# Holding loads behind x, moving all weight conversions behind the spectrum, and giving GpSimd both filter sums, in the opening of a Fourier mixer with a SoLU layer

## The chip, the cores and the metric

The kernel runs on one core of a Trainium2 chip. A core has five engines that each work through their own instructions in order: TensorE (PE; its weight loads are shown as PEld), VectorE (DVE), ScalarE (ACT), GpSimd (POOL) and SyncE (SP), which here only issues DMAs. SP, ACT and POOL issue the DMAs of this kernel; those of POOL are prepared by POOL's own instructions, so they take its time. Sixteen DMA engines carry the data. The metric is device time in microseconds (us), the median of several runs.

## The reference

Everything is float32 but the two weight matrices, which arrive as float64 words.

```python
X = np.fft.rfft(x, axis=1)                   # x: (8, 3136, 256)
y = np.fft.irfft(X * (filt_r + 1j * filt_i)[None], n=3136, axis=1)
t = y.reshape(25088, 256)
h = t @ w_in                                 # w_in: (256, 1024)
solu = h * softmax(h)
ln = (solu - mean(solu)) / sqrt(var(solu) + 1e-6) * g_ln
out = ln @ w_out                             # w_out: (1024, 256)
```

## The kernel before

The transform of 3136 = 49 x 64 points is done by matrix products. For one example: a first product with `wf_t` (L233) over the 49-point part, whose result goes to a scratch tensor `d1` in DRAM to be rearranged; then the spectrum, seven units of up to two residue pairs, each with forward products (L308, tile `pb`), the product with the filter (`multiply`, L329 to L331), inverse products (L308, tile `pc`) and a store to the scratch tensor `d2`; then a product back with `wi_t` (`back`, L404), which leaves `y`. The token layer works on `y` in steps of a hand-written order (`step`): products with `w_in_sb` (L754), the softmax and the products with `w_out_sb` (L885). Examples 1 to 7 are transformed between these steps by the table `PLAN`.

The change lies in the opening, which handles example 0 alone and prepares the weights before step 0 can run. All of it is under a manual schedule: program order is the order on each engine.

- `fetch_x` loads x in eight pieces of four columns. Half 0 (48 rows a piece, and the last row by itself) goes through SP, half 1 (49 rows, reversed) through POOL, each with runs of 4 KB and 1 KB. `begin(0)` and `begin(1)` (raw float64 words of two weight quarters, 512 KB each) stand between them on POOL; the tables `de` and filter rows `f` of the first eight pairs follow (`load_tables`, two sets of nine DMAs).
- After each piece's first product ACT copies it out and it is stored to `d1`: 96 rows by ACT, 4 by SP.
- `idle_row(5)` puts five products that nothing reads ahead of the spectrum. Each is a full float32 product and shows as two PE instructions. They need the first set of tables. One more idle product stands before each unit's inverse, and `idle_row(14)` after the last.
- SP fetches the units' `d1` rows (`t2`) once `d1` has landed; the last two units' are fetched by POOL.
- In `multiply` DVE forms two products from PSUM per part; the difference of part 0 is DVE's, the sum of part 1 is GpSimd's (L331).
- `load_float64` turns one quarter of the weights (128 x 512) into float32: eight DVE instructions, for `w_in` an ACT and a GpSimd product besides, and an addition, on GpSimd but for the last quarter, where it is a ninth DVE instruction. Quarters 0 and 1 are done early; 2 to 7 after the spectrum. `weight_sums(w_in_sb)` (L152) then forms the combined quarters.
- SP loads the `d2` rows back (`t4`, L358), then x of example 1, and stores the filters to `f_dram`.
- Step 0 starts with `product(0, 1)`, `keep` (ACT, L764), `product(0, 2)` and `finish` (DVE, L778). It ends with `prepare_w_out` (L691 to L709). `pair_sums(0)` and the x loads of later pieces stand on POOL in front of it.

The `raw` tiles have five buffers, `power`, `pt`, `pr` and `pi` two each.

Of the kernel before, what the change touches and what calls it, by code (L numbers as in the profile page):

```python
# [9 lines left out]
FP32 = mybir.dt.float32  # L10
# [84 lines left out]
def kernel(  # L95
# [315 lines left out]
    with ExitStack() as st:  # L411
# [13 lines left out]
        def load_float64(dst, raw, negate, share, add=nc.gpsimd.tensor_tensor):  # L425


            lo, hi = raw[:, :, 0], raw[:, :, 1]
            power = wpool.tile([P, 512], I32, name="power", tag="power", bufs=2)
            frac = dst.bitcast(I32)  # L430
            ts, stt = nc.vector.tensor_scalar, nc.vector.scalar_tensor_tensor
            ts(out=lo, in0=lo, scalar1=8, scalar2=None, op0=ALU.logical_shift_right)
            rest = lo.bitcast(FP32)
            ts(out=power, in0=hi, scalar1=20, scalar2=0x7FF, op0=ALU.logical_shift_right,
               op1=ALU.bitwise_and)
            ts(out=power, in0=power, scalar1=896.0, scalar2=0.0, op0=ALU.subtract, op1=ALU.max)
            if negate:
                ts(out=power, in0=power, scalar1=255.0, scalar2=None, op0=ALU.min)
                ts(out=power, in0=power, scalar1=23, scalar2=-2 ** 31, op0=ALU.logical_shift_left,
                   op1=ALU.bitwise_or)  # L440
            else:
                ts(out=power, in0=power, scalar1=255.0, scalar2=2.0 ** 23, op0=ALU.min, op1=ALU.mult)
            stt(out=power, in0=hi, scalar=-2 ** 31, in1=power, op0=ALU.bitwise_and,
                op1=ALU.bitwise_xor)
            ts(out=frac, in0=hi, scalar1=0xFFFFF, scalar2=3, op0=ALU.bitwise_and,
               op1=ALU.logical_shift_left)
            nc.vector.tensor_tensor(out=frac, in0=frac, in1=power, op=ALU.bitwise_or)


            if share:  # L450
                nc.scalar.mul(rest, lo, 2.0 ** -44)
                nc.gpsimd.tensor_tensor(out=rest, in0=rest, in1=power.bitcast(FP32), op=ALU.mult)
            else:
                stt(out=rest, in0=lo, scalar=2.0 ** -44, in1=power.bitcast(FP32), op0=ALU.mult,
                    op1=ALU.mult)
            add(out=dst, in0=dst, in1=rest, op=ALU.add)
# [82 lines left out]
        fetch_x(0, 0, NCH, 0, N1 - 1, nc.sync.dma_start)  # L539
        fetch_x(0, 0, NH, N1 - 1, 1, nc.sync.dma_start)  # L540
        for i in range(pieces):
            if i:
                fetch_x(0, NCH * i, NCH, 0, N1 - 1, nc.sync.dma_start)
# [12 lines left out]
        def idle(out):  # L556

            nc.tensor.matmul(out=out, lhsT=tables[0][0][:, 0, 0].rearrange("p u q -> p (u q)"),
                             rhs=filters[0][0][:, 0], start=True, stop=True)
# [5 lines left out]
        idle_row(5, "idle")  # L565

        def convert(j):
            load_float64(weights[j][0], raws.pop(j), negate=j < 4, share=j < 4,
                         add=(nc.vector if j == 7 else nc.gpsimd).tensor_tensor)

        for j in range(2):
            convert(j)
# [9 lines left out]
        for i in range(1, units - 2):  # L582
            sp.fetch(i, nc.sync.dma_start, spare_piece(i - 1))
            if i == 3:
                load_tables(8, NP - 8, nc.sync.dma_start)
        for i in range(2):
            start(i)
            tables_back(4 * i, 4)
        for i in range(units):
# [4 lines left out]
            sp.multiply(i, 0, nc.vector.tensor_tensor)  # L594
            sp.multiply(i, 1, nc.gpsimd.tensor_tensor)
            pss = [ps_t.tile([P, 2, C], FP32, name=f"pc_0_{i}_{u}", tag="t") for u in range(2)]
            idle(pss[0])
            sp.inverse(i, pss)
            sp.store(i, nc.scalar.dma_start)
            if i == 0:  # L600
                nc.gpsimd.dma_start(out=wi_t, in_=wi_dram)
                nc.gpsimd.dma_start(out=wq_t, in_=wq_dram)
                nc.gpsimd.dma_start(out=wb_t[:, 0:N1], in_=wb_dram)
                nc.gpsimd.dma_start(out=g_sb, in_=moe_g_ln.rearrange("(k p) -> p k", p=P))
            elif i == 1:
                for last_one in (units - 2, units - 1):
                    sp.fetch(last_one, nc.gpsimd.dma_start, spare_piece(last_one - 1))
# [559 lines left out]
```

## Time and profile before

| | |
|---|---|
| runs, median (lowest to highest) | 1599.01 us (1598.26 to 1602.79) |
| profiled execution: span | 1598.0 us; the page gives no other time for it |
| granted TensorE clock, mean | 0.997 |
| busy: PE, DVE, ACT, POOL | 97%, 82%, 57%, 74% |
| first product of example 0 starts / spectrum starts | 11.76 / 43.42 us |
| back starts / step 0's first product | 82.78 / 97.05 us |

The span is 1.0 us below the median of the runs. Starts are counted from the start of the span. In a timeline a line has the start, the time taken, the engine, the line of the kernel, the instruction and what it writes and reads; the brackets hold the idle time before it and what ended that. A DMA line of SPq, ACTq or POOL is the issue alone, not the transfer.

### The profile page before, as it was taken

What the parts mean: (1) busy time and instruction counts of PE and PEld (TensorE: products, weight loads), DVE (VectorE), ACT (ScalarE), POOL (GpSimd) and SP (SyncE); (2) the same over time, 40 slices, a digit from 0 to 9 for tenths busy, and PEclk for the clock granted to TensorE, in tenths of its full rate; (3) what the DMA queues carried; (4) which work ended last, traced back from release to release, by engine and by line L of the source; (5) the groups of instructions that cost most, each with busy time, mean ns of one, the idle gap of its engine ahead of it and who ended that gap; (6) DMA issues with size and microseconds to landing.
All of it is one profiled execution on the core that took longest, in us unless ns stands there. A gap on an engine that the chain in (4) does not pass through costs nothing. (4 is left out here: it accounts for less than half of the span.)

```text
span 1598.0 us, 37061 instructions
## 1 busy us (share of the span) xinstructions
PE 1548.0 (97%) x12828; PEld 1055.5 (66%) x12828; DVE 1310.2 (82%) x2639; ACT 915.8 (57%) x1825; POOL 1177.0 (74%) x1371
## 2 busy tenths in 40 slices
PE   5998999999999999999999999999999999999997
PEld 1463567666666676667766776667776777777777
DVE  1887888998998889888988889987898777777773
ACT  2245655656565656565566656665555666665653
POOL 4555986688768867886778877886866867677775
PEclk8999999999999999999999999999999999999999
DMA  9989978776987588766886678766784544343434
GB/s 261 288 272 261 262 214 236 215 228 175 247 245 231 157 230 238 230 177 169 235 240 195 166 196 256 209 183 174 222 220 127 134 125 127 96 113 99 113 103 115
DMA packets 343804, 311.14 MB, mean 195 GB/s; under 512 B 27835, under 2 KB 310100, under 8 KB 343620
## 3 DMA queue, kind: packets, MB, share of 16 engines
q1 hardware_dynamic: 271476, 170.45, 40.4%
q0 software_dynamic: 33744, 98.81, 20.6%
q10 hardware_dynamic: 38400, 39.53, 8.2%
q8 instruction: 104, 1.70, 0.5%
q14 instruction: 80, 0.65, 0.1%
HBM read 124.51 MB, written 81.40 MB: 129 GB/s over the span
## 5 line engine op out<-in xcount | busy, mean ns | idle before, releaser
L885 PEld LDWEIGHTS o<-w_out_sb,solu_t 128*128 128x128 f32 x3136 | 381.5, 192 | 50.2 <-issue 43.2
L885 PE MATMUL o<-w_out_sb,solu_t 128*128 128x128 f32 x3136 | 401.5, 276 | 3.8 <-DVE ot L905 3.1
L754 PE MATMUL m<-w_in_sb,s 128*128 128x512 f32 x784 | 397.9, 608 | 2.1 <-ACT h L764 1.4
L885 PEld LDWEIGHTS o<-w_out_sb,u 128*128 128x128 f32 x2352 | 305.9, 191 | 140.7 <-issue 104.0
L802 DVE SCALAR_TENSOR_TENSOR h<-e,rsum,h 128x1024 f32<-128x1024 f32 x196 | 321.2, 1639 | 6.9
L885 PE MATMUL o<-w_out_sb,u 128*128 128x128 f32 x2352 | 310.4, 275 | 3.0 <-POOL u L733 2.1
L754 PE MATMUL m<-w_in_sb,y 128*128 128x512 f32 x588 | 306.6, 604 | 3.0 <-DVE h L775 2.1
L764 ACT COPY h<-m 128x512 f32<-128x512 f32 x294 | 173.2, 589 | 201.8 <-PE m L754 193.6
L901 ACT ACTIVATE ot<-o,rs_t 128x128 f32<-128x128 f32 x392 | 143.2, 366 | 248.0 <-PE o L885 244.6
L733 POOL TENSOR_TENSOR u<-solu_t 128x512 f32<-128x512 f32 x98 | 133.5, 1362 | 178.3 <-DMA solu_t<-turn 157.0
L810 ACT ACTIVATE h<-h,nmu 128x1024 f32<-128x1024 f32 x196 | 224.6, 1146 | 47.0 <-DVE turn L818 37.4
L818 DVE STREAM_TRANSPOSE turn<-h 128x1024 f32<-128x1024 f32 x196 | 243.1, 1241 | 3.1
L778 DVE CUSTOM_DVE_ANT_0 h<-m,h 128x512 f32<-128x512 f32 x196 | 133.2, 679 | 131.6 <-ACT h L764 94.5
L786 ACT ACTIVATE e<-h,nmax 128x1024 f32<-128x1024 f32 x196 | 225.1, 1148 | 20.1 <-DVE h L802 18.8
L733 POOL TENSOR_TENSOR u<-solu_t,u 128x512 f32<-128x512 f32 x98 | 147.6, 1506 | 94.0 <-PE o L885 94.0
L754 PEld LDWEIGHTS m<-w_in_sb,s 128*128 128x128 f32 x784 | 127.9, 190 | 88.0 <-issue 68.3
L905 DVE SCALAR_TENSOR_TENSOR ot<-o,rs_t,ot 128x128 f32<-128x128 f32 x299 | 103.7, 347 | 73.8 <-ACT ot L901 55.6
L733 POOL TENSOR_TENSOR u<-u,solu_t 128x512 f32<-128x512 f32 x98 | 152.0, 1551 | 15.2 <-PE o L885 7.2
L733 POOL TENSOR_TENSOR solu_t<-solu_t,solu_t 128x512 f32<-128x512 f32 x98 | 161.8, 1651 | 0.9
L754 PEld LDWEIGHTS m<-w_in_sb,y 128*128 128x128 f32 x588 | 96.3, 190 | 98.1 <-issue 54.7
L733 POOL TENSOR_TENSOR s<-y 128x128 f32<-128x128 f32 x196 | 97.9, 500 | 0.5
L381 PEld LDWEIGHTS py<-wb_t,t 50*64 50x64 f32 x3584 | 57.6, 134 | 42.9 <-issue 22.5
(126 smaller groups left out, 2001.6 us busy)
## 6 DMA issues: line engine op xcount, KB each, us to landing
solu_t<-turn SPq DMA_DIRECT2D x780, 128.0 KB
out_dram<-ot SPq DMA_DIRECT2D x196, 128.0 KB
t<-d POOLq DMA_DIRECT2D x112, 200.0 KB, 6.8
d<-x POOLq DMA_DIRECT2D x100, 200.0 KB, 5.0
f<-f_dram POOLq DMA_DIRECT2D x39, 512.0 KB, 8.2
t<-d ACTq DMA_DIRECT2D x37, 512.0 KB
d<-g POOLq DMA_DIRECT2D x36, 512.0 KB, 4.9
x<-in_x_dram SPq DMA_DIRECT2D x112, 98.0 KB
```

The costliest lines, as they stand in the source:

```text
L381: nc.tensor.matmul(out=views[g][64 * h:64 * h + 64, cb, i, :], lhsT=t4[rows, i, c0:c0 + 64], rhs=wb_t[rows, 0:N1], start=True, stop=True)
L733: nc.gpsimd.tensor_tensor(out=out, in0=in0, in1=in1, op=op)
L754: nc.tensor.matmul(out=ms[j, bank], lhsT=lhsT, rhs=w_in_sb[:, w, :], start=m in (1, 2, 7), stop=True, skip_group_check=True)
L764: nc.scalar.copy(out=h_half(k, i), in_=ms[j, 0])
L778: nc.vector.tensor_tensor_reduce(out=h_half(k, i), in0=ms[j, bank], in1=h_half(*kept), scale=1.0, scalar=sofar, op0=ALU.add, op1=ALU.min, ...
L786: nc.scalar.activation(out=e, in_=hs[k], func=AFT.Exp, bias=nmaxs.pop(k)[:, 1:2], scale=-1.0, accum_out=esum)
L802: nc.vector.scalar_tensor_tensor(out=solu, in0=e, scalar=rsum, in1=solu, op0=ALU.mult, op1=ALU.mult, accum_out=nmu)
L810: nc.scalar.activation(out=solu, in_=solu, func=AFT.Square, bias=nmu, scale=-float(DFF), accum_out=variances[g][:, i:i + 1])
L818: nc.vector.transpose(out=turns[g][:, :, i, :], in_=solus[k].rearrange("p (f j) -> p f j", j=32))
L885: nc.tensor.matmul(out=pos[p, bank], lhsT=lhs[:, f, :], rhs=w[:, f, :], start=f == 0 and (m in (1, 2, 7) or alone), stop=True, skip_group_ ...
L901: nc.scalar.activation(out=out_half(p, *to)[0], in_=pos[p, 0], func=AFT.Copy, scale=rs)
L905: nc.vector.scalar_tensor_tensor(out=ot, in0=pos[p, bank], scalar=rs, in1=out_half(p, *kept)[0], op0=ALU.mult, op1=ALU.add)
```

## The change

Loads: half 1 of x goes in pieces of 48 rows too, its last row through SP; the tables wait, by a GpSimd copy of one column (`once_landed`), for piece 4 of x, and the first raw words for the first `t2` rows. Raw words 0 to 4 are begun in the spectrum, 5 to 7 between conversions. All `t2` rows go through SP; three tables move from POOL to ACT, `g_sb` goes behind the spectrum.

PE: two products on a constant come before x; `idle_row` becomes 10 instead of 5 and 7 instead of 14, and the idle product within a unit has half the columns.

DVE and GpSimd: both filter sums go to GpSimd. All eight conversions come behind the spectrum, each as six DVE instructions (`split`), two ACT products and a GpSimd addition and multiplication (`join`); the last four follow the product back.

```diff
-        def load_float64(dst, raw, negate, share, add=nc.gpsimd.tensor_tensor):
...
+        def split_float64(raw):
+            lo, hi = raw[:, :, 0], raw[:, :, 1]
+            power = wpool.tile([P, 512], I32, name="power", tag="power", bufs=2)
...
+            ts(out=power, in0=power, scalar1=255.0, scalar2=2.0 ** 23, op0=ALU.min, op1=ALU.mult)
+            nc.vector.scalar_tensor_tensor(out=power, in0=hi, scalar=-2 ** 31, in1=power,
+                                           op0=ALU.bitwise_and, op1=ALU.bitwise_xor)
+            ts(out=hi, in0=hi, scalar1=0xFFFFF, scalar2=0x100000, op0=ALU.bitwise_and, op1=ALU.bitwise_or)
+            return power
+        def join_float64(dst, raw, power, sign):
+            lo, hi = raw[:, :, 0], raw[:, :, 1]
+            rest = lo.bitcast(FP32)
+            nc.scalar.mul(dst, hi, sign * 2.0 ** -20)
+            nc.scalar.mul(rest, lo, sign * 2.0 ** -44)
+            nc.gpsimd.tensor_tensor(out=dst, in0=dst, in1=rest, op=ALU.add)
+            nc.gpsimd.tensor_tensor(out=dst, in0=dst, in1=power.bitcast(FP32), op=ALU.mult)
...
-            fetch_x(1, NCH * i, NCH, 0, N1, nc.gpsimd.dma_start)
-            if i in (4, 7):
-                begin(i // 7)
+            for h, dma in ((0, nc.sync.dma_start), (1, nc.gpsimd.dma_start)):
+                fetch_x(h, NCH * i, NCH, 0, N1 - 1, dma)
+                if i == 0:
...
+        once_landed(rows_x[0:NR, NCH * 4, 0:1])
         load_tables(0, 4, nc.gpsimd.dma_start)
         load_tables(4, 4, nc.gpsimd.dma_start)
+        warm = y[:, 0, 0:512]
+        nc.vector.memset(warm, 1.0)
+        for n in range(2):
+            nc.tensor.matmul(out=ps_t.tile([P, 512], FP32, name=f"warm_{n}", tag="t"), lhsT=warm[:, 0:P],
+                             rhs=warm, start=True, stop=True)
...
-        idle_row(5, "idle")
+        idle_row(10, "idle")
...
-        for j in range(2):
-            convert(j)
...
-        for i in range(1, units - 2):
+        for i in range(1, units):
             sp.fetch(i, nc.sync.dma_start, spare_piece(i - 1))
...
+        once_landed(sp.t2s[0][:, 0, 0:1])
+        begin(0)
...
-            sp.multiply(i, 0, nc.vector.tensor_tensor)
+            sp.multiply(i, 0, nc.gpsimd.tensor_tensor)
             sp.multiply(i, 1, nc.gpsimd.tensor_tensor)
...
-            idle(pss[0])
+            idle(pss[0][:, 0, :])
...
-            for j in {2: (2,), 3: (3, 4), 4: (5,), 5: (6,)}.get(i, ()):
-                begin(j)
-        idle_row(14, "idler")
+            if i < 4:
+                begin(i + 1)
+        idle_row(7, "idler")
...
-        convert(2)
-        convert(3)
-        begin(7)
-        convert(4)
-        weight_sums(w_in_sb)
-        for j in (5, 6, 7):
-            convert(j)
+        for j in range(3):
+            split(j)
+            join(j)
+            begin(j + 5)
+        split(3)
         for ch in range(pieces):
             for cb in range(KD):
                 back(0, ch, cb, nc.scalar.copy)
+            if ch == 1:
+                join(3)
+                weight_sums(w_in_sb)
+        for j in range(4, 8):
+            split(j)
+            join(j)
```

More of the change, by code (lines that the diff above doesn't have):

```diff
@@ L423, in load_words @@
             return raw
[L425 removed]
+        def split_float64(raw):
             lo, hi = raw[:, :, 0], raw[:, :, 1]
             power = wpool.tile([P, 512], I32, name="power", tag="power", bufs=2)
[L430 to L431 removed]
+            ts = nc.vector.tensor_scalar
             ts(out=lo, in0=lo, scalar1=8, scalar2=None, op0=ALU.logical_shift_right)
[L433 removed]
             ts(out=power, in0=hi, scalar1=20, scalar2=0x7FF, op0=ALU.logical_shift_right,
@@ L436, in load_float64 @@
             ts(out=power, in0=power, scalar1=896.0, scalar2=0.0, op0=ALU.subtract, op1=ALU.max)
[L437 to L456, printed above, removed]
+            ts(out=power, in0=power, scalar1=255.0, scalar2=2.0 ** 23, op0=ALU.min, op1=ALU.mult)
[10 more added lines that the diff above has]
+            nc.gpsimd.tensor_tensor(out=dst, in0=dst, in1=power.bitcast(FP32), op=ALU.mult)
         filters, tables = {}, {}
@@ L537, with once_landed @@
         pieces = NH // NCH
-        fetch_x(0, 0, NCH, 0, N1 - 1, nc.sync.dma_start)
-        fetch_x(0, 0, NH, N1 - 1, 1, nc.sync.dma_start)
         for i in range(pieces):
-            if i:
-                fetch_x(0, NCH * i, NCH, 0, N1 - 1, nc.sync.dma_start)
-            fetch_x(1, NCH * i, NCH, 0, N1, nc.gpsimd.dma_start)
-            if i in (4, 7):
-                begin(i // 7)
+            for h, dma in ((0, nc.sync.dma_start), (1, nc.gpsimd.dma_start)):
+                fetch_x(h, NCH * i, NCH, 0, N1 - 1, dma)
+                if i == 0:
+                    row, at = N1 * h + N1 - 1, N2 * (N1 - 1) + NH * h
+                    nc.sync.dma_start(
+                        out=rows_x[row:row + 1, ::-1 if h else 1, :],
+                        in_=x[0, at:at + NH, :].rearrange("(o n) c -> o n c", o=1))
+        seen = small.tile([P, 1], FP32, name="seen", tag="seen")
+        def once_landed(ap):
+            nc.gpsimd.tensor_copy(out=seen[0:ap.shape[0]], in_=ap)
+        once_landed(rows_x[0:NR, NCH * 4, 0:1])
         load_tables(0, 4, nc.gpsimd.dma_start)
         load_tables(4, 4, nc.gpsimd.dma_start)
+        warm = y[:, 0, 0:512]
[3 more added lines that the diff above has]
+                             rhs=warm, start=True, stop=True)
         for i in range(pieces):
@@ L558, in idle @@
             nc.tensor.matmul(out=out, lhsT=tables[0][0][:, 0, 0].rearrange("p u q -> p (u q)"),
-                             rhs=filters[0][0][:, 0], start=True, stop=True)
+                             rhs=filters[0][0][:, 0, 0:len(out.shape) - 1], start=True, stop=True)
         def idle_row(count, name):
@@ L563, in idle_row, with split, join @@
                 idle(ps_h.tile([P, 2, C], FP32, name=f"{name}_{j}", tag="h"))
-        idle_row(5, "idle")
-        def convert(j):
-            load_float64(weights[j][0], raws.pop(j), negate=j < 4, share=j < 4,
-                         add=(nc.vector if j == 7 else nc.gpsimd).tensor_tensor)
-        for j in range(2):
-            convert(j)
+        idle_row(10, "idle")
+        powers = {}
+        def split(j):
+            powers[j] = split_float64(raws[j])
+        def join(j):
+            join_float64(weights[j][0], raws.pop(j), powers.pop(j), -1.0 if j < 4 else 1.0)
         def start(i):
@@ L600 @@
             if i == 0:
[L601 to L607, printed above, removed]
-            for j in {2: (2,), 3: (3, 4), 4: (5,), 5: (6,)}.get(i, ()):
-                begin(j)
-        idle_row(14, "idler")
+                nc.scalar.dma_start(out=wi_t, in_=wi_dram)
+                nc.scalar.dma_start(out=wq_t, in_=wq_dram)
+                nc.scalar.dma_start(out=wb_t[:, 0:N1], in_=wb_dram)
+            if i < 4:
+                begin(i + 1)
+        idle_row(7, "idler")
         rows_t4 = pools["r"].tile([P, NH, C], FP32, name="t4_0", tag="r")
@@ L621 @@
                 in_=f[0:rows, at:at + n].rearrange("p i k c -> p i (k c)"))
-        convert(2)
-        convert(3)
-        begin(7)
-        convert(4)
-        weight_sums(w_in_sb)
-        for j in (5, 6, 7):
-            convert(j)
+        nc.gpsimd.dma_start(out=g_sb, in_=moe_g_ln.rearrange("(k p) -> p k", p=P))
+        for j in range(3):
[3 more added lines that the diff above has]
+        split(3)
         for ch in range(pieces):
```

## The prediction

> **What bounds the kernel now.** I read the page first: TensorE is busy 97% of the span, so outside the opening the time is TensorE's work, which this change leaves alone. What counts is when step 0 gets going. Next I read the table of windows for the opening (after the stretch: its length, then PE, PEld, DVE, ACT, POOL busy, granted clock, DMA share, GB/s).
>
> ```profile
> 0.00:10.00 10.00, 0.00 (x0) 0.00 (x0) 0.06 (x1) 0.00 (x0) 6.28 (x12) 1.00 0.83 171
> 10.00:20.00 10.00, 8.24 (x14) 3.04 (x15) 0.00 (x0) 3.58 (x4) 2.66 (x4) 1.00 1.05 220
> 20.00:30.00 10.00, 8.27 (x20) 2.96 (x18) 5.77 (x13) 5.80 (x6) 3.71 (x7) 1.00 1.02 388
> 90.00:100.00 10.00, 10.00 (x72) 8.23 (x72) 9.73 (x17) 5.09 (x11) 3.68 (x4) 1.00 0.55 175
> ```
>
> The DMA engines are busy nearly throughout, at 171 to 220 GB/s while x arrives. DVE is nearly idle for 20 us and full at 90 to 100. Then I followed the timeline.
>
> ```profile
> 36.30 7.19 PE L558 MATMUL idle<-f,de 128*128 128x512 f32 x10 [8.02 <-DMA f<-in_filt_r_dram]
> 37.28 0.40 SPq L298 DMA_DIRECT2D t<-d  x1
> 43.42 1.11 PE L308 MATMUL pb<-t,de 64*64 64x256 f32 x16
> 70.66 12.28 PE L558 MATMUL idler<-f,de 128*128 128x512 f32 x28
> 71.20 0.34 ACTq L350 DMA_DIRECT2D d<-g  x1
> 73.78 1.35 POOL L456 TENSOR_TENSOR w_in_sb<-w_in_sb,raw 128x512 f32<-128x512 f32 x1
> 73.91 1.51 DVE L434 TENSOR_SCALAR power<-raw 128x512 int32<-128x512 int32 x1
> 75.74 10.16 SPq L358 DMA_DIRECT2D t<-d  x16
> 82.78 14.43 PE L404 MATMUL py<-wi_t,t 100*128 100x98 f32 x128
> 103.34 0.69 DVE L456 TENSOR_TENSOR w_out_sb<-w_out_sb,raw 128x512 f32<-128x512 f32 x1
> 104.05 1.88 PE L754 MATMUL m<-w_in_sb,s 128*128 128x512 f32 x4
> 104.33 0.56 POOL L1132 DMA_DIRECT2D turn_t<-turn_tbl  x1 [2.63 <-DVE w_out_sb L456]
> ```
>
> The spectrum starts when the idle row, itself held by the tables, is through. The back products start when the second idle row (70.66 + 12.28 = 82.94) is through. Yet the end of the opening is neither: DVE converts without a break from 68.09 to 104.03, the last copy of the back products being done at 97.25 + 0.49 = 97.74. From 104.05 PE is busy 16.0 of 16.0 us, so a delay there is passed on; only between 120 and 170 does it idle 6 us.
>
> **Part 1, x and tables.** x is 98 rows of 32 KB, 3.21 MB: at 215 GB/s (the windows' upper row) 14.9 us from 2.2 us. By then ACT's stores to `d1` have joined, 0.4 MB a piece, 1 us each at the 388 GB/s of the third window; five or six lie before the last piece, so it lands at 22.5 instead of 25.6 (issue 11.99 plus 13.6). Bounds 17 (no sharing) and 25.6. A product of 1.7 us and a copy of 1.0 follow, so the last `d1` store is issued near 25.5 instead of 29.73. Issue to landed was 7.5 us there (37.28) and 4.5 for the last `d2` store (71.20 to 75.74); I take 6, and `t2` is fetched from 31.5 and lands 5.5 later (5.2 for such a fetch on POOL), at 37.
>
> The tables wait on POOL for piece 4, with nothing else queued behind. Nine issues take 0.77 + 8 x 0.57 = 5.3 us, but their 1.3 MB follow the last x pieces on the same queue: 22.5 + 1.3 MB at 230 GB/s + 2 = 30 (bounds 26 and 36). PE has then idled over 4 us. The granted clock was 0.78 in 30 to 31 us and 0.50 after, the last product having ended at 28.28; the old row of ten instructions took 7.19 us, the first four at 1.07, the others at 0.43. Ten more at 0.43 make 11.5: the spectrum starts at 41.5, 1.9 earlier (bounds 31 and 43.4). The `warm` products buy nothing here, since x paces; without that cover they save 2.6 us (six slow L233 products at 0.86). SP's second row load is 0.4 us of issue, hidden by the transfers queued ahead of it. The 1 MB of raw words that leaves this stretch is already out of the 22.5.
>
> One page of the Trainium skill speaks for more. "DMA: Bandwidth & Descriptors" (Why a DMA increments its semaphore by 16 and not by 1) says that a transfer runs on the largest number of engines up to 16 that divides the leading counts: 7 for 49 rows, 16 for 48. The fourth window, where 49-row loads of x run nearly alone, agrees, with a share of 0.55. As an estimate from that page, x would land near 12 us and the spectrum start near 31. In the first windows, however, the share is 0.83 to 1.05 already, so I go by 215 GB/s.
>
> **Part 2, spectrum.** A sum takes DVE 0.61 and GpSimd 1.28, or 1.38 from start to start (38.41 to 39.80). POOL now sets the pace: twelve full sums 16.6, two small ones 1.7 (0.77 each before), four `begin` issues 2.5, so 20.8 us; with 2.5 ahead (forward and two multiplications) and 2.1 behind (inverse, copy) it is 25.4, against 71.20 - 43.42 = 27.8. That is 2.4 less. PE needs about 2.5 us a unit with the halved idle product, POOL 2.8 to 3.4. If `t2` of units 5 and 6, now behind the third tables on SP, comes late, 1 us is lost; SP's issues (12.3 us to unit 4 before) put them at about 50, needed at 56. ACT's three table issues are 1.0 us, covered by the 14.5 us that it waits for PE in these copies. Last `d2` store: 66.9; landed 4.5 later, 71.4.
>
> **Part 3, back.** The idle row of 14 instructions ends at 72.5. The first `t4` lands about 4.6 us after its issue (4.5 for `wi_t`, 5.2 for 512 KB on POOL): 76.0, where before it hid behind the row. So back starts 6.8 earlier, which is 1.9 + 2.4 + 2.5. But PE has idled 3.5 us by then. If the clock falls, the first 5 us run at half speed and cost 2.5; between 0 and 2.5 I take 1.2. `join(3)` stands among ACT's copies: 1.25 us of ACT with two PSUM tiles to cover it, 0.8. The last copy ends at 97.74 - 6.8 + 2.0 = 93.0.
>
> **Part 4, conversions.** A split's six DVE instructions follow each other at 0.34, 0.48, 0.46, 0.46, 0.61 and 0.46: 2.8 us, where eight took 3.9 to 4.4. A join is 1.25 of ACT (two in 1.23, L451) and 2.7 of GpSimd (38.41 to 41.08). Less DVE work, then, but a chain over three engines. `split(0)` to `split(3)` and the sums of `w_in` fit before the back products end, and so do splits 4 and 5; the issue of `g_sb`, 0.9 on POOL ahead of `join(0)`, is hidden by that join's wait for ACT. Then DVE stops: `power` has two buffers, so `split(6)` needs `join(4)`, whose ACT products are queued behind all sixteen back copies. From the last copy: join 4 by 4.0; split 6 by 8.6 (2.5 of its own, 2.1 of waits for join 5 on GpSimd); join 6 by 12.65, with split 7 beside it until 13.1; join 7 by 17.1. On ACT, step 0's `keep` stands behind join 7; on POOL `pair_sums` does, whose second sum is ready at 18.2.
>
> The 2.1 is what the pair at 73.78 and 73.91 shows: L434, 0.43 us alone, took 1.51 while GpSimd added, ending 0.3 after it. Without such waits the tail is 13.3. "SBUF - State Buffer" (Who interferes with whom), in the Trainium skill, states it as a lock: a fast-mode or two-input DVE instruction and a GpSimd one shut each other out for a whole instruction. That speaks against this change; as an estimate from the page, with GpSimd shut out in its turn, the tail is up to 18. It exempts the multiplications from PSUM, and L330 is indeed 0.68 beside GpSimd's sums.
>
> **Sum.** `product(0, 6)` starts at 93.0 + 18.2 = 111.2, against 104.05: +7.1. POOL's x loads go from 104.88 to about 112.7, +7.8. Of the 6 us that PE idles later I let 1 to 2 be taken back: +6. The span of 1598.0 is 1.0 below the median of 1599.0; added to the median, 1605.0.
>
> **Rivals.** (a) Faster: x, `d1` and the first tables, 7.8 MB, stream at the 388 GB/s of the best window. They are in at 22.3, a warm idle row of 20 x 0.43 = 8.6 brings the spectrum at 31, 10.5 before mine, and the clock holds at the back products: 6 - 10.5 - 1.2 = -5.7, 1593.3. It decides from a spectrum start before 35.5. For it: half 1 of x no longer comes in 49 rows. Against it: the busy DMA engines and the 11.5 us of the row when cold. (b) No change: the two port waits and the cold clock cost nothing, 6 - 3.8 - 1.2 = +1.0, 1600. (c) Slower still: raw words 5 to 7 (1.6 MB at 230 GB/s, 6.8 us) run beside the `t4` loads, and back is paced by them; half of it shows, +3.4, 1608.4.
>
> **Numbers.** 0.3%, 4.8 us, is about what a measurement can tell from no change. Mine 0.40, (c) 0.12, (a) 0.20, (b) 0.28. So slower 0.52, same 0.28, faster 0.20. The range takes (a)'s and (c)'s values and beyond (c) 1.3 for a wholly cold start of back, 1 for late `t2` and 2.3 for tables later than 30: 1594 to 1613. Of the cases of one sign alone, mine with (c) spans 1602 to 1613.
>
> **What would show it.** Right: spectrum at 41 or so, `idle` still behind the tables, POOL the last releaser of the `pc` products, DVE idle between splits 5 and 6, and `h` L764 of step 0 after the last L451-like product, at about 108. Wrong: a spectrum before 36, back copies ending before 87, or join 7 less than 14 us behind them.

## The result, and the profile after

The changed kernel takes 1644.7 us (1641.8 to 1645.2), against 1598.6 us for the kernel before in the same comparison: a ratio of 1.0271, 95% interval 1.0248 to 1.0294. The profiled execution has a span of 1640.0 us, 42.0 more than before, and a mean granted clock of 0.978 (0.997 before). The forecast was slower by 6 us; the sign was right and the size was not.

The windows of the opening come first (length, PE, PEld, DVE, ACT, POOL busy, granted clock, DMA share, GB/s), the same stretches as in the prediction and one more:

```profile
0.00:10.00 10.00, 4.48 (x5) 1.58 (x6) 0.55 (x2) 0.75 (x1) 5.02 (x12) 0.93 0.82 181
10.00:20.00 10.00, 10.00 (x18) 3.60 (x17) 0.00 (x0) 4.13 (x5) 4.53 (x9) 0.73 0.99 272
20.00:30.00 10.00, 8.11 (x19) 3.01 (x18) 0.00 (x0) 4.50 (x5) 5.72 (x11) 0.95 1.00 341
90.00:100.00 10.00, 10.00 (x48) 10.00 (x48) 5.41 (x8) 3.54 (x7) 5.35 (x5) 0.50 1.01 255
```

More is moved while x comes in (272 GB/s in the second window, 220 before). The fourth window shows the damage: DVE, 9.73 busy before, is half idle, PE is full, and the clock is 0.50. The timeline gives the milestones:

```profile
28.16 10.52 PE L561 MATMUL idle<-f,de 128*128 128x512 f32 x20 [1.89 <-DMA f<-in_filt_i_dram]
36.22 0.40 SPq L298 DMA_DIRECT2D t<-d  x1
40.19 1.12 PE L308 MATMUL pb<-t,de 64*64 64x256 f32 x16 [1.51 <-DMA t<-d]
54.46 5.29 SPq L298 DMA_DIRECT2D y<-d  x3
62.47 2.01 PE L308 MATMUL pb<-y,de 64*64 64x256 f32 x16 [8.03 <-DMA y<-d]
76.72 6.28 PE L561 MATMUL idler<-f,de 128*128 128x512 f32 x14
77.26 0.34 ACTq L350 DMA_DIRECT2D d<-g  x1
86.13 2.85 PE L404 MATMUL py<-wi_t,t 100*128 100x98 f32 x16 [3.14 <-DMA t<-d]
89.44 24.21 PE L404 MATMUL py<-wi_t,t 100*128 100x98 f32 x112 [0.46 <-ACT y L407]
113.44 3.67 PE L761 MATMUL m<-w_in_sb,y 128*128 128x512 f32 x4
118.69 1.50 DVE L432 TENSOR_SCALAR power<-raw 128x512 int32<-128x512 int32 x1 [13.21 <-POOL w_out_sb L447]
131.11 1.26 POOL L447 TENSOR_TENSOR w_out_sb<-w_out_sb,power 128x512 f32<-128x512 f32 x1
132.55 3.40 DVE L698 TENSOR_SCALAR w_out_sb<-w_out_sb,g_sb 128x128 f32<-128x128 f32 x16
```

Read downwards. The spectrum starts 3.2 us earlier than before. Unit 4's forward products wait 8.0 us for their input, which SP asked for at 54.46 (49.54 before), so the last `d2` store is 6.1 us later. The back products take 27.5 us where they took 14.4. The conversions end 18 us behind the last copy of `y`; DVE stood 13.2 us, until 118.69, waiting for join 4. The scaling of `w_out` (L698, L691 before), which needs the last conversion, starts at 132.55 in place of 104.70: 27.9 us lost in the opening. The other 14 us are lost later: from that line to the end of the span it is 1507.5 us, and 1493.3 before.

This table holds the milestones of the kernels run. "Steady" is from the scaling to the end of the span.

| kernel | spectrum | last d2 store | back starts | last back copy ends | scaling | steady | ratio (95%) |
|---|---|---|---|---|---|---|---|
| before | 43.4 | 71.2 | 82.8 | 97.7 | 104.7 | 1493.3 | |
| after | 40.2 | 77.3 | 86.1 | 114.2 | 132.6 | 1507.5 | 1.0271 (1.0248 to 1.0294) |
| e1 | 39.5 | 79.3 | 88.3 | 114.3 | 132.7 | 1514.7 | 1.0251 (1.0215 to 1.0286) |
| e2 | 40.9 | 75.1 | 89.7 | 117.8 | 136.1 | 1511.3 | 1.0289 (1.0268 to 1.0310) |
| e3 | 41.0 | 76.4 | 84.1 | 112.7 | 131.1 | 1511.9 | 1.0245 (1.0221 to 1.0268) |
| e4 | 40.6 | 78.0 | 86.3 | 114.9 | 123.6 | 1512.6 | 1.0235 (1.0218 to 1.0252) |
| b1 | 43.1 | 72.5 | 84.1 | 99.0 | 105.8 | 1491.2 | 0.9999 (0.9978 to 1.0020) |
| b2 | 42.0 | 69.7 | 81.3 | 96.3 | 103.2 | 1488.4 | 0.9994 (0.9971 to 1.0017) |
| e5 | 42.9 | 70.7 | 80.9 | 108.3 | 111.1 | 1489.4 | 1.0101 (1.0072 to 1.0129) |
| e6 | 44.1 | 72.3 | 83.8 | 98.8 | 105.8 | 1490.9 | 1.0008 (0.9989 to 1.0027) |
| s1 | 43.0 | 71.1 | 82.7 | 97.7 | 104.6 | 1508.7 | 1.0124 (1.0098 to 1.0149) |
| s2 | 42.1 | 74.9 | 83.4 | 111.8 | 130.2 | 1497.9 | 1.0181 (1.0160 to 1.0203) |
| s3 | 42.5 | 82.6 | 94.2 | 110.3 | 130.1 | 1491.8 | 1.0147 (1.0128 to 1.0165) |
| s4 | 40.3 | 79.1 | 87.5 | 116.0 | 134.4 | 1498.3 | 1.0185 (1.0154 to 1.0216) |
| p1 | 44.6 | 72.8 | 84.3 | 99.3 | 106.3 | 1494.1 | 0.9997 (0.9979 to 1.0016) |
| d1 | 39.1 | 73.0 | 84.5 | 99.5 | 106.4 | 1493.0 | 1.0015 (0.9994 to 1.0036) |
| c1 | 40.2 | 71.1 | 82.7 | 97.7 | 105.1 | 1499.5 | 1.0000 (0.9980 to 1.0021) |
| c2 | 41.6 | 74.5 | 86.2 | 101.7 | 108.5 | 1497.0 | 1.0022 (1.0004 to 1.0041) |
| d2 | 39.2 | 68.2 | 80.8 | 95.9 | 102.8 | 1501.3 | 0.9998 (0.9981 to 1.0014) |
| c3 | 41.2 | 75.1 | 87.3 | 103.4 | 110.0 | 1501.3 | 1.0020 (1.0000 to 1.0039) |

One profiled execution stands behind each row, and the ratio behind it comes from several timed runs; "steady" differs by up to some 10 us between executions of kernels whose timed runs agree (1493.3 before; 1499.5 to 1501.3 in c1, d2 and c3, at ratios of 0.9998 to 1.0020). The way from the spectrum's start to the last `d2` store differs too where nothing in the program does: up to there `after`, e1 and e4 are the same program, s2 and s3 too but for the place of one tile, and it took 37.1, 39.8, 37.4, 32.8 and 40.1 us in them. In the kernels with the order of before (before, b2, e5, e6, s1, p1) it was 27.8 to 28.2. So a difference of 3 us in the spectrum between single profiles of the new order shows nothing by itself.

### The profile page after: what moved, and what is told of

It is laid out like the page before. It is cut to its first block, busy times and chain, and to the rows that moved or that the text cites. A ratio compares the mean times of both kernels' runs of the same rounds, so it can differ in the third digit from the quotient of the medians.

```text
span 1640.0 us, 37080 instructions
## 1 busy us (share of the span) xinstructions
PE 1573.9 (96%) x12828; PEld 1075.3 (66%) x12828; DVE 1305.0 (80%) x2616; ACT 919.2 (56%) x1837; POOL 1186.8 (72%) x1380
## 5 line engine op out<-in xcount | busy, mean ns | idle before, releaser
L892 PEld LDWEIGHTS o<-w_out_sb,solu_t 128*128 128x128 f32 x3136 | 381.8, 192 | 57.2 <-issue 43.1
L892 PEld LDWEIGHTS o<-w_out_sb,u 128*128 128x128 f32 x2352 | 306.4, 192 | 140.6 <-issue 105.1
L809 DVE SCALAR_TENSOR_TENSOR h<-e,rsum,h 128x1024 f32<-128x1024 f32 x196 | 316.2, 1613 | 6.9
L740 POOL TENSOR_TENSOR u<-solu_t 128x512 f32<-128x512 f32 x98 | 138.6, 1414 | 201.9 <-DMA solu_t<-turn 150.4
L817 ACT ACTIVATE h<-h,nmu 128x1024 f32<-128x1024 f32 x196 | 224.8, 1147 | 53.4 <-DVE turn L825 41.6
L740 POOL TENSOR_TENSOR u<-solu_t,u 128x512 f32<-128x512 f32 x98 | 146.0, 1490 | 82.7 <-PE o L892 82.6
L740 POOL TENSOR_TENSOR solu_t<-solu_t,solu_t 128x512 f32<-128x512 f32 x98 | 165.2, 1686 | 0.9
L381 PEld LDWEIGHTS py<-wb_t,t 50*64 50x64 f32 x3584 | 57.6, 134 | 42.9 <-issue 20.9
```

The costliest lines, as they stand in the source:

```text
L381: nc.tensor.matmul(out=views[g][64 * h:64 * h + 64, cb, i, :], lhsT=t4[rows, i, c0:c0 + 64], rhs=wb_t[rows, 0:N1], start=True, stop=True)
L740: nc.gpsimd.tensor_tensor(out=out, in0=in0, in1=in1, op=op)
L809: nc.vector.scalar_tensor_tensor(out=solu, in0=e, scalar=rsum, in1=solu, op0=ALU.mult, op1=ALU.mult, accum_out=nmu)
L817: nc.scalar.activation(out=solu, in_=solu, func=AFT.Square, bias=nmu, scale=-float(DFF), accum_out=variances[g][:, i:i + 1])
L892: nc.tensor.matmul(out=pos[p, bank], lhsT=lhs[:, f, :], rhs=w[:, f, :], start=f == 0 and (m in (1, 2, 7) or alone), stop=True, skip_group_ ...
```

## The experiments

### The back products and the clock: e1, e5

```diff
-        idle_row(7, "idler")        # e1, in the kernel after
+        idle_row(11, "idler")
-        idle_row(14, "idler")       # e5, in the kernel before
+        idle_row(7, "idler")
```

> The changed kernel with 11 instead of 7 idle products behind the spectrum, nothing else. Theory 'clock': the product back ran its 24 us at the halved clock because PE had idled 3.1 us before it, and its own products do not raise the clock. Then the row ends at about 86.4, back starts at 86.5 at most and lasts 14.5 us: its last copy at about 101.5 instead of 114.2, and the span about 12 us shorter, 1628 to 1632. Rival 'transfers': back is paced by the t4 rows that share the DMA engines with raw words 5 to 7. Then the copies stay 1.7 us apart and the time stays within 2 us of the changed kernel's.

> The kernel before with 7 instead of 14 idle products behind the spectrum. Theory 'clock': the row ends at 76.8, t4 lands at 79 to 80, the gap is 2 to 4 us, the clock falls, and the back products, which do not raise it, last 28 us instead of 15: last copy at 107 to 108 instead of 97.7; but DVE's conversions end at 104 anyway, so the time grows by 4 to 8 us. Rival 'short cold start': the clock is back after 5 us; the back products start 3 us earlier, end near 97 and the time is the same within 2 us.

The timeline of e5 shows the row and the back products:

```profile
70.11 6.28 PE L558 MATMUL idler<-f,de 128*128 128x512 f32 x14
80.93 26.83 PE L404 MATMUL py<-wi_t,t 100*128 100x98 f32 x128 [4.54 <-DMA t<-d]
```

So seven fewer products that nobody reads are enough, in the kernel before, to make the 128 back products take 26.8 us in place of 14.4, with the granted clock at 0.50 from 81.8 to 109.1. PE had waited 4.5 us for the first `t4`. The scaling came 6.4 us later, the other conversions covering the rest, and the timed runs rose by 1.0% by their ratio (medians 1611.8 us and 1600.6). The profiled execution was the fastest of them (span 1600.5, 2.5 above the kernel before); why the others lost more than the 6.4 is open, as they have no trace.

In e1 the longer row did reach up to the back products, and the products ran warm at first, but not the rest. Its timeline:

```profile
88.31 1.92 PE L404 MATMUL py<-wi_t,t 100*128 100x98 f32 x16
90.27 0.66 ACT L445 ACTIVATE raw<-raw 128x512 f32<-128x512 int32 x1
91.34 22.44 PE L404 MATMUL py<-wi_t,t 100*128 100x98 f32 x112 [1.11 <-ACT y L407]
```

ACT held `join(2)` (until 90.9) and `join(3)` (until 96.0) while two PSUM tiles waited for its copies. PE stalled 1.1 us, until 91.34; the clock fell at 93.5, 2.2 us later, and stayed down until 117.4, behind the last back product. This stall is the only one there; a stall of 0.83 us in c3's back products did not lose the clock. The theory that the row was too short was therefore half right: a longer row alone did not do it, and ACT's joins, which caused the stall, are the likely other half.

### The end of the conversions: e4

```diff
-            nc.scalar.mul(dst, hi, sign * 2.0 ** -20)
-            nc.scalar.mul(rest, lo, sign * 2.0 ** -44)
+            if sign > 0:
+                nc.vector.tensor_scalar(out=dst, in0=hi, scalar1=sign * 2.0 ** -20, scalar2=None, op0=ALU.mult)
+                nc.vector.tensor_scalar(out=rest, in0=lo, scalar1=sign * 2.0 ** -44, scalar2=None, op0=ALU.mult)
+            else: ...
```

> The changed kernel with the two products of joins 4 to 7 on DVE instead of ACT, so that they do not queue behind the sixteen copies of back. Theory 'chain behind back': the 18.4 us from the last copy to the first scaling of w_out shrink, since joins 4 to 7 run beside back: four conversions of 3.7 us DVE and 2.2 us of port waits each from 99.5 end near 124, so the scaling starts near 124 to 126 instead of 132.6 and the time falls by 6 to 9 us. Rival 'port': DVE and GpSimd shut each other out so much that the tail keeps its length; no change within 2 us.

From the last back copy to the scaling it is 8.7 us in place of 18.4, so DVE's 13.2 us wait was the join behind ACT's copies, as the prediction said. The time against its three neighbours of the same comparison (1.0245 to 1.0289) fell by 0.1 to 0.5%, less than the 9 us of the milestone and about the width of the intervals, so the timed runs hardly show it.

### Both sums on GpSimd: e6

```diff
-            sp.multiply(i, 0, nc.vector.tensor_tensor)
+            sp.multiply(i, 0, nc.gpsimd.tensor_tensor)
```

> The kernel before with both filter sums on GpSimd, nothing else. Theory: DVE loses 0.6 us a unit, GpSimd's two sums of 1.38 a unit keep within the 3.0 us of a unit, so the spectrum ends within 1 us of before (71.2 for the last store), DVE starts its conversions 1 to 3 us earlier and the time is the same within 3 us. Rival 'GpSimd paces': the last store comes 2 us later or more.

From spectrum start to last `d2` store it is 28.2 us (27.8 before). The sums cost nothing on GpSimd and bring nothing.

### Unit 4's wait: e2, e3, b1, b2, s4

e2 issues raw words 0 to 4 behind the whole spectrum; e3 puts SP's third tables behind all `t2` rows; both are edits of the kernel after. b1 and b2 put one reordering each into the kernel before. s4 drops the hold of the tables from s2 (below).

```diff
-            if i < 4:                           # e2
-                begin(i + 1)
+        for j in range(5):                      # behind the loop over the units
+            begin(j)
-            if i == 3:                          # e3
+            if i == units - 1:
                 load_tables(8, NP - 8, nc.sync.dma_start)
-                nc.gpsimd.dma_start(out=wi_t, in_=wi_dram)    # b1, wq_t and wb_t too
+                nc.scalar.dma_start(out=wi_t, in_=wi_dram)
-        for i in range(1, units - 2):           # b2, and the two fetches on GpSimd left out
+        for i in range(1, units):
-        once_landed(rows_x[0:NR, NCH * 4, 0:1])  # s4
```

> The changed kernel with raw words 0 to 4 begun behind the spectrum instead of inside it. Theory 'raw words': their 2.6 MB take the DMA engines from the third tables and the t2 rows, so unit 4's rows land at 62. Without them its forward products start by about 54, the spectrum ends 8 us earlier, and the conversions start late instead (the words land 10 to 16 us after). Rival 'order on SP': unit 4's rows are late because they stand behind nine table loads on SP; then forward 4 still starts after 60.

> The changed kernel with all seven t2 fetches on SP ahead of the third tables. Theory 'order on SP': unit 4's rows land early; if the tables are then in time (they are 1.5 MB, as much as three units' rows), forward 4 starts by about 54. Theory 'raw words': the tables are now the late ones, and the stall before forward 4 stays at 6 us or more, only its releaser changes to a table.

> The kernel before with only the three small table loads (wi, wq, wb) moved from POOL to ACT. Theory 'shared counters': DMAs of SP and ACT take eight completion counters in turn, so an issue waits for the transfer eight places earlier, whichever of the two queues it was on. Then ACT's copies in the spectrum stop for SP's filter rows, SP's fetch of unit 4 comes 2 us or more later than 49.5, and since every later DMA shifts by three places the steady part may be slower as well, by up to 10 us. Rival 'too small to matter': 127 KB in three loads; the spectrum and the time stay within 2 us.

> The kernel before with only the t2 rows of units 5 and 6 moved from POOL to SP, behind unit 4's. Theory 'order on SP': units 5 and 6 come later than the 58.2 us of before, by 3 us or more, and the last d2 store with them. Theory 'shared counters': nothing in the opening but two places of shift later on; the opening stays within 2 us and the whole within 10.

> s2 without the copy that holds the tables 0 to 7 behind x's fifth piece (one line less). If the hold is what makes unit 4's inputs late (8.0 us wait for t2 in the kernel after, the tables' last rows and SP's fetch of unit 4 5 us later than before), the wait falls below 4 us and the last d2 store comes 4 to 6 us earlier; x may land 1 to 3 us later, so 0 to 5 us less than s2 in all. If the two queues for x or the faster start are the cause, the wait stays at 6 to 8 us.

No one of these orders is shown to be the cause by itself. Unit 4's forward products start at 59.3 in e2 (wait 4.2 us) and 59.0 in e3, against 62.5: 3 us each, less than like programs differ by. In e3 they no longer wait for their input; PE waits 4.4 us ahead of them for ACT's copy, which stands behind ACT's table issues. The times of b1 and b2 are those of the kernel before. In s4 unit 4 starts at 64.1. So it was neither the hold alone nor the order of SP's queue alone; d1 and d2 below take it up again.

The traces do show where the wait begins. In the kernel after and in e1, e2, e4, s2, s3 and s4 SP issues unit 4's fetch at 52.6 to 62.3; in the other kernels, but for e3's new order, at 46.6 to 51.1. SP was held by landings of older transfers: in the kernel after by one of a filter row (2.3 us just ahead of the fetch, 5.9 us earlier), in e2 by ACT's first `d2` store, which the fetch neither reads nor overwrites (3.4 us). e2 had no raw words in the way and its DMA engines were busy 0.61 of the stretch from 48 to 52, yet it issued at 54.39, as the kernel after did at 54.46. So the raw words, if anything, cost part of the time from issue to product (8.0 us, and 4.9 in e2), and the late issue itself is set by landings that SP's queue waits for. ACT's three table issues were held likewise, and PE with them:

```profile
51.76 1.07 ACT L346 COPY g<-pc 128x512 f32<-128x512 f32 x2 [3.35 <-DMA f<-in_filt_r_dram]
```

No run changes these waits alone, so how much of unit 4's wait is theirs and how much is traffic stays open.

### The part that does not touch the opening: s1, s2, p1

The kernel after and e1 to e4 had a steady part 14 to 21 us longer, and SP's queue took more time for the same bytes. The change has one line that outlives the opening:

```diff
+        seen = small.tile([P, 1], FP32, name="seen", tag="seen")
```

`small` is the pool ahead of all later ones. In the compiled programs its four buffers take 128 bytes of each partition, and the later tiles lie 128 bytes further on. In the kernel before, nearly all tiles of the bulk transfers start at multiples of 512 bytes.

```diff
+        seen = small.tile([P, 1], FP32, name="seen", tag="seen")   # s1, in the kernel before
+        nc.gpsimd.memset(seen, 0.0)
+        seen = small.tile([P, 1], FP32, name="seen", tag="seen", bufs=8)   # p1: as s1, 256 bytes
-        seen = small.tile([P, 1], FP32, name="seen", tag="seen")   # s2, in the kernel after
+        seen = fpool.tile([P, 1], FP32, name="seen", tag="seen")
```

> The kernel before, with one thing of the change alone: the one-column tile `seen` is taken from the pool `small` (one memset on GpSimd writes it, nothing else uses it). In every variant of the kernel after so far the part behind the first w_out scaling took 1507.5 to 1514.7 us and the SP queue's packets 700 to 708 engine-us of time, against 1488 to 1493 and 643 to 646 in every variant of the kernel before. Theory 'place': the pool `small` lies ahead of all later pools, so the new tile shifts their addresses, and the SP queue's packets take longer: +13 to +20 us, queue time about 700. Rival 'backlog': the steady part is longer because the late opening leaves the DMA queues behind: no change here, 1598 to 1602.

> The kernel after, with `seen` taken from the opening's own pool `fpool`, which is given back before the steady pools are made; every instruction stays. Theory 'place': the steady part goes back to 1488 to 1493 us, the SP queue's time to about 645, and the whole to 1622 to 1630 (the opening's +28 stays). Rival 'backlog': 1640 to 1647 as the kernel after.

> As s1, with eight buffers of `seen` in place of four: in the compiled program the later tiles then lie 256 bytes further on a partition than in the kernel before, where s1 moved them by 128 bytes and cost 1.2% (span 1613.3, SP queue 43.6% of 16 engines' span). In the kernel before nearly all tiles that bulk transfers read or write start at multiples of 512 bytes. Theory 'multiple of 256': a whole multiple of 256 costs nothing, 1597 to 1602 and a queue share of 40 to 41%. Rival 'any move': half or all of s1's cost, 1608 to 1620.

The page's line for SP's queue (packets, MB, share of 16 engines' span) in the kernel before, in s1 and in p1, in this order:

```profile
q1 hardware_dynamic: 271476, 170.45, 40.4%
```

```profile
q1 hardware_dynamic: 271476, 170.45, 43.6%
```

```profile
q1 hardware_dynamic: 271476, 170.45, 40.3%
```

The same packets and bytes, but 703 us of each engine's time in s1 against 646 before (share times span). By size, the 200,320 packets of 512 bytes take 37.0 ns each on average in s1 and in the kernel after, and 32.8 before, in p1 and 32.9 in s2; the packets of 4 KB of GpSimd's queue have a median of 174 ns in s1 and 159 before and in p1. s1 costs 1.24% alone. A move by 256 bytes costs nothing, so it is the place modulo 256, not the tile or the memset. s2 gives 0.9% of the 2.7% back. Set side by side by the starts of one DVE instruction of each step's layers (L802, 196 of them), the loss builds up over most of the span: 4.3 us at the 14th, 8.1 at the 45th, 11.9 at the 61st, 15.3 at the 141st.

The Trainium skill has a rule that bears on it: "DMA: Bandwidth & Descriptors" (How a descriptor splits into AXI transactions) says that a transaction starts at a multiple of 256 bytes and covers at most 256, so that a descriptor that does not start at one needs another and fetches bytes that it drops. By the page's count, 512 bytes at an odd multiple of 128 take 20 beats in place of 16, an estimate of 25% more. The runs agree on the boundary (128 costs, 256 does not) and not on the size: 13% for 512 bytes.

### Eight conversions or six: s3, c1

s3 is s2 with all the joins' multiplications on DVE and 14 idle products. c1 is the kernel after without the move of the bulk tiles (`seen` takes the place of a tile of the same pool), with s3's idle row, raw words 0 and 1 loaded behind the tables and converted before the spectrum, and the multiplications of joins 4 to 7 on DVE.

```diff
-            nc.scalar.mul(dst, hi, sign * 2.0 ** -20)      # s3; in c1 for sign > 0 alone
-            nc.scalar.mul(rest, lo, sign * 2.0 ** -44)
+            ts(out=dst, in0=hi, scalar1=sign * 2.0 ** -20, scalar2=None, op0=ALU.mult)
+            ts(out=rest, in0=lo, scalar1=sign * 2.0 ** -44, scalar2=None, op0=ALU.mult)
-        idle_row(7, "idler")
+        idle_row(14, "idler")
+        for j in range(2):                                 # c1, behind load_tables(4, 4, ...)
+            begin(j)
+        for j in range(2):                                 # c1, ahead of the spectrum
+            split(j)
+            join(j)
+        for j in (2, 3): ...                               # c1: 2 to 7 ahead of back in program order
```

> s2 with two edits: all joins' two multiplications by a constant on VectorE in place of ScalarE, so that ScalarE has only the back copies there, and 14 products in the second idle row in place of 7. Theory 'clock': the back products then start right behind a row that has brought the clock up and nothing stalls them, so that the 32 products take 15 us in place of 28, and the tail behind them about 9 in place of 18: first w_out scaling near 108 to 112, 16 to 22 us less than s2. Rival 'other waits': VectorE, which gets 16 products more, or POOL holds the back or the clock falls all the same: 0 to 8 us less than s2.

> The kernel after with three things put back: raw words 0 and 1 loaded behind the tables and converted ahead of the spectrum, in the new form (2 to 7 behind it, in the order of the kernel before), no tile that moves the others (`seen` shares a tile's place), and 14 idle products in the second row; the joins of 4 to 7 have their multiplications on VectorE, those of 0 to 3 on ScalarE, all ahead of the back products. x on two queues, the hold of the tables, both sums on POOL, and the placing of the tables and of units 5 and 6's inputs stay. Theory 'eight conversions do not fit behind': s3 took 50.5 us on VectorE from the spectrum's end (79.4) to the w_out scaling (130.1), 5.7 a conversion; six take 36 to 38, so scaling at 112 to 116, and 1604 to 1609 in all. Rival 'unit 4's stall or the cold back remain the bound': 1612 or more.

s3's back products, in its timeline, and then the window over them (columns as above):

```profile
82.07 12.29 PE L562 MATMUL idler<-f,de 128*128 128x512 f32 x28
94.19 10.86 PE L404 MATMUL py<-wi_t,t 100*128 100x98 f32 x96
```

```profile
94.00:110.00 16.00, 15.27 (x130) 14.63 (x129) 13.02 (x24) 7.47 (x16) 6.39 (x5) 1.00 0.89 226
```

and the window over those of the kernel after:

```profile
86.00:114.00 28.00, 27.41 (x129) 27.02 (x130) 14.48 (x25) 9.74 (x20) 7.69 (x7) 0.52 0.81 241
```

Warm, the same products take 15.3 us of PE; at half clock 27.4. Yet s3's scaling comes no earlier than s2's, and the expected 16 to 22 us became 5 or 6. One reason is that its spectrum ended 7.7 us later than s2's in the profile (last `d2` store at 82.6 and 74.9), with nothing changed ahead of it; from the first conversion to the scaling it is 50.7 us, and 58.5 in s2. Why it is not less, its DVE timeline says. This is the middle of one of its conversions, with GpSimd's addition beside it:

```profile
84.23 1.39 POOL L447 TENSOR_TENSOR w_in_sb<-w_in_sb,raw 128x512 f32<-128x512 f32 x1 [2.76 <-DVE raw L446]
84.39 1.51 DVE L432 TENSOR_SCALAR power<-raw 128x512 int32<-128x512 int32 x1
85.94 1.38 DVE L434 TENSOR_SCALAR power<-power 128x512 int32<-128x512 int32 x1
```

L432 takes 0.42 us when GpSimd is not adding. Each join's two GpSimd products so hold two DVE instructions for 2.0 us together, and a conversion takes 5.7 us on DVE (3.6 in c1, from 87.27 to 90.85, where none of the two was held). From 79.4 until its last conversion, DVE does little else but add the `w_in` sums: eight conversions in this form take 45 to 50 us behind the spectrum. c1 does six there; its scaling starts at 105.1 and its time is that of the kernel before, 1.0000 of it, with a spectrum that starts 3.2 us earlier.

### What the earlier spectrum is worth: d1, c2, d2, c3

d1 puts x's part alone into the kernel before, c2 gives GpSimd the three tables and units 5 and 6's rows back in c1, and d2 and c3 move raw words 2 to 6 back by up to two units in d1 and c1.

```diff
+            for h, dma in ((0, nc.sync.dma_start), (1, nc.gpsimd.dma_start)):   # d1
+                fetch_x(h, NCH * i, NCH, 0, N1 - 1, dma)      # and the last rows on SyncE
-                nc.scalar.dma_start(out=wi_t, in_=wi_dram)    # c2
+                nc.gpsimd.dma_start(out=wi_t, in_=wi_dram)
-            for j in {2: (2,), 3: (3, 4), 4: (5,), 5: (6,)}.get(i, ()):   # d2, c3
+            for j in {4: (2, 3), 5: (4, 5, 6)}.get(i, ()):
```

> The kernel before with the x part alone: x's 48-row pieces on two queues and both last rows as loads of their own on SyncE; nothing is held, and every other transfer and all conversions stay as they were. If x is what brought the spectrum forward in the kernel after (40.2 in place of 43.4), it starts near 40 to 41.5 here too, and since conversions 2 to 7 on VectorE set the end, 0 to 3 us of that comes out: 1596 to 1600. If the hold of the tables and raw words made the room, the spectrum stays at 43 to 44 and the time at 1600.

> c1 with wi_t, wq_t, wb_t and the inputs of units 5 and 6 back on GpSimd's queue. SyncE's and ScalarE's transfers share eight completion counters in program order; in the kernel after SyncE's fetch of unit 4 waits for the counter of a filter load four issues before it, in the kernel before for one six issues before. If that is what makes unit 4 late, its wait falls from 8 to below 5 us and the spectrum (start to last d2 store) from 32 to 37 us in the kernels after to 28 to 30: 3 to 6 us less than c1. If the traffic of the stretch is the cause, it is within 2 us of c1.

> d1 (the kernel before with the x part alone) with raw words 2 and 3 issued behind unit 4 and 4 to 6 behind unit 5, in place of 2 behind unit 2, 3 and 4 behind unit 3, 5 and 6 behind units 4 and 5. In d1 the spectrum started at 39.1 and its last d2 store still came at 73.0, as in the kernel before (43.4 and 71.2). Theory 'traffic': the 1.5 MB of raw words 2 to 4, about 4.5 us at the 300 to 330 GB/s of this stretch, hold up unit 4's input; without them the last d2 store comes at 68 to 70, and the whole is 2 to 4 us less than d1, unless raw 2 then comes too late for VectorE (wanted from 68). Rival 'order of SyncE's queue': unit 4's input is behind the third tables whatever the raw words do: 72 to 74, the same time as d1.

> c1 with the same five raw loads placed as in d2. c1's spectrum ran from 40.2 to 71.1. By 'traffic' the last d2 store comes 2 to 4 us earlier and the time is 0 to 3 us less than c1 and than the kernel before (the best version that the experiments point to); by the rival it is c1's time.

Unit 4's forward products in d1 and then in d2:

```profile
55.87 2.01 PE L308 MATMUL pb<-y,de 64*64 64x256 f32 x16 [4.00 <-DMA y<-d]
```

```profile
52.63 1.12 PE L308 MATMUL pb<-y,de 64*64 64x256 f32 x16 [0.59 <-DVE pr L331]
```

x's part alone makes the spectrum start 4.3 us earlier, and unit 4's input then makes PE wait: the last `d2` store comes 1.8 us later than before. With the raw words behind it, the wait for the input is gone and the store comes at 68.2, 4.8 us before d1's. This speaks for the raw words holding up the input in d1, on one profile each; the timed runs show no difference (1.0015 and 0.9998), and in c1 the same move brought nothing (75.1, 4.0 later than c1, with a spectrum that started 1.0 later). c2 is no faster than c1, but it says nothing on its expectation, that ACT's table DMAs make SP wait for newer transfers: in c1 SP issues unit 4's fetch at 47.16 already, and its products do not wait for it. And the 2 to 4 us that d2 has at the scaling do not show in its time, 0.9998 (0.9981 to 1.0014). No version beat the kernel before by more than the interval.

## Why the prediction was right or wrong, step by step

**The first premise failed.** "Outside the opening the time is TensorE's work, which this change leaves alone" leaves out that the steady steps are also fed by DMA, and that a line of the diff moves every later tile. This term was not in the sum at all; s1 and s2 put it at 0.9 to 1.2%, 14 to 20 us. The diff showed the line, and the page showed SP's queue at 40.4%; the two were not put together.

**Part 1 was right in its result, and partly by luck.** Spectrum at 41.5 predicted, 40.2 measured. x was not at 22.5: GpSimd's pieces, the last issued at 5.57, had landed 12.3 us later, by 17.8, near the bound of 17 without sharing (its 215 GB/s lies between the windows' 171 and 220; no row shows it). PE set the pace in place of x: it was busy 10.00 of 10.00 us from 10 to 20 at a granted clock of 0.73, so the first products ran partly at half speed, the `warm` products having ended at 5.26. The last `d1` store was issued at 28.0 (25.5 predicted), `t2` was fetched at 36.2 (31.5) and landed at 40.2 (37). The tables were in at 28 and not 30 (no row shows the "+ 2" in that sum), and the row took 10.5 us and not 11.5; it does not decide, as the first `t2` landed 1.5 us after it was through. So an early x and a late `t2` offset each other. Rival (a), which needed a start before 35.5, fell, and so did the estimate from the page on engine counts: x near 12 was 5.8 us too early, the spectrum at 31 9 us.

**Part 2 failed.** The spectrum was to take 25.4 us and took 37.1. "If `t2` of units 5 and 6 comes late, 1 us is lost" had the right wait at the wrong unit, and too small: unit 4 waited 8.0 us. In the runs with the same code up to there the spectrum took 32.8 to 40.1 us and unit 4's wait was 6.1 to 9.2, all above the prediction. Two things were left out. The prediction moved loads from the idle row into the spectrum and counted their bytes only where they left ("already out of the 22.5"), not where they went. GpSimd's queue moved 2.62 MB between 40 and 62 us, 1.67 before. And it took SP's and ACT's issues to be free when their turn came, with ACT's three at "1.0 us, covered": SP asked for unit 4's input at 54.46, held by the landing of a filter row, and ACT's three took 2.8 us (48.87 to 51.71) and PE waited 2.6 us for the copy behind them. e2, without the raw words in the way, still waited 4.2 us. How the 8.0 us divide between the two is open. The 2.4 us of gain by GpSimd's pace did not come either: e6 has 28.2 us. Nor was POOL the last releaser of the `pc` products: behind the wait the units follow each other in 2.5 to 2.6 us (`d2` stores issued at 68.36, 70.94, 73.41 and 75.97), less than the 2.8 to 3.4 given for POOL, and it is ACT's copies that those products wait for.

**Part 3: the right mechanism, mis-sized.** From the last `d2` store to the back products it was 9.1 predicted and 8.9 measured. But the cold clock, "the first 5 us run at half speed", at most 2.5, took all 128 products: 12.6 us more. The Trainium skill, "TensorE: Matmul & The Clock Gate" (Part 1), gives a busy window of about 3.4 us for the clock to come up; by that, as an estimate, it would have been up by 90. It came up at 117.8. These products do not bring it up: PE was busy 27.4 of 28.0 us in the window over them, at 0.52. In s3 they kept a clock that was up. Why they do not raise it is open. The last copy so came at 114.2, not 93.0.

**Part 4 was right, but for one clause.** From the last back copy to join 7's end 17.1 predicted, 18.2 measured (131.11 + 1.26 - 114.18), and the wait of split 6 for join 4 was where it was put. `keep` and `pair_sums` did not stand behind join 7, though: they ran at 116.3 and 114.3, between the joins. So it is the scaling of `w_out` and not `product(0, 6)` that the tail held.

**The sum.** Delay at the end of the opening: +27.9 against +7.1, of which unit 4's wait and the spectrum's start 6.1 - 2.7 (the shorter way from the last store to the back products), the back products and their copies 13.1 (28.05 - 14.96), and the tail 11.4 (18.4 - 7.0), which the prediction had nearly so. "1 to 2 taken back" did not happen: step 1's first L809 instruction is 29.6 us late. Then the steady part adds 14.2, which goes when the tiles lie as before. In timed runs: 2.71% in all; 1.81 without the moved tiles (s2); 1.47 with a warm back and the joins on DVE (s3); 0.00 with two conversions early again (c1).

**The rivals.** (b), no change, supposed the clock and the port waits to cost nothing; both cost. (c), the raw words beside the `t4` loads, put the moved raw words beside the wrong transfer: the back products awaited `t4` 3.1 us (3.5 predicted), and if the raw words hold up anything, it is unit 4's rows. The range ended at 1613 because the cold start was bounded by 2.5, late `t2` by 1, and the steady part was given nothing.

## What to carry to other kernels

When a load is moved out of one stretch, count its bytes in the stretch that it goes to, and look up which older transfers its queue waits for before it can issue the next; and when a helper tile is added, ask where the pool puts it and what moves behind it: 128 bytes cost this kernel about as much as the whole cold stretch of its opening, and a move by 256 cost nothing. Before shortening a row of warming products, look at what follows: if those products cannot raise the clock by themselves, the price is the whole stretch at half speed, not a start-up. And work that moves to an engine's free stretch (conversions before the spectrum) is worth keeping there, even if the new form has fewer instructions.

## What the runs showed that was not expected

- The place of a tile modulo 256 bytes: 512-byte packets take 37.0 ns in place of 32.8 at an odd multiple of 128, and the kernel 1.24% (1.0098 to 1.0149).
- Products of 100 x 98, with PE busy 93 to 100% of the stretch, did not raise the granted clock from 0.50 in 20 to 28 us in eight kernels (after, e1 to e5, s2, s4), though they held it at 1.00 in s3. It rose with the 128 x 512 products behind them, at 109.1 to 120.0. In e1 it fell 2.2 us after a stall of 1.1 us; in c3 a stall of 0.83 us did not lose it.
- A DVE instruction of 0.42 us beside a GpSimd addition took 1.37 to 1.52 us, to two instructions in nearly every conversion: 5.7 us in place of 3.6.
- With raw words 0 and 1 loaded early, the last `d2` store came at 70 to 75 us, whether the spectrum started at 39 or 45; only d2, with the later raw words moved back, had it at 68, and c3, with the same move, at 75.
- The same program up to the spectrum's end took 32.8 to 40.1 us for it in five profiles, with unit 4's wait at 6.1 to 9.2 us.
- By the profile, an issue on SP is held by a transfer that it has nothing to do with: in e2, 3.4 us by the landing of a `d2` store of ACT.
